# A retention block and a leaky-ReLU feed-forward block: the decay tables read from 8 rows, the first weights moved up in the load order, the first dense step cut by batch

## The chip, the cores and the metric

The kernel runs on one core of one Trainium2 chip. The core has a matrix engine (TensorE, "PE" in the profile, with its weight loads "PEld"), a vector engine (VectorE, "DVE"), a scalar engine (ScalarE, "ACT"), GpSimd ("POOL") and SyncE ("SP"). Each runs its own list of instructions in order, and they wait for each other through semaphores. Transfers between the main memory (HBM) and the on-chip memory (SBUF) run on 16 DMA engines; here SP issues nearly all of them and ACT issues two. Matrix products are summed in PSUM[...]. The metric is the device time of one execution, in microseconds, as the median of several runs.

## The reference

The inputs are q, k and v in float32, each of 4 batches, 8 heads, 768 positions and 64 dimensions, and w_in of 512 x 2048 and w_out of 2048 x 512 in float64. The kernel turns the weights into float32 itself.

```python
gamma = 1.0 - 2.0 ** (-5.0 - np.arange(H))
for t in range(S):
    state = gamma * state + k[t] (outer) v[t]        # per batch and head
    y[t] = scale * (q[t] @ state)
x = y as (B*S, H*D)                                  # 3072 x 512
h = x @ w_in
out = maximum(0.01 * h, h) @ w_out
```

The recurrence is computed in six chunks of 128 positions. Within a chunk, a product of q and k gives 128 x 128 scores, which are masked below the diagonal and multiplied with v; a factor of gamma to the power of the position goes onto v before (the table of v's decay) and onto the result after (the table of q's decay). Across chunks a state is carried.

## The kernel before, in words

The two dense layers take nearly all of the time. They are done chunk by chunk (4 batches x 128 positions = 512 tokens at a time) and, over the hidden dimension, in four units of 512. Most of them use a seven-product scheme for 2 x 2 blocks (Strassen's), and the later chunks a second level of it. The order of all instructions on every engine is written out by hand in the program; no planner decides it. Each engine takes its instructions in the order in which the program states them.

The change touches only the opening, the first chunk of attention and the first dense unit (about the first 17 us of the profile). What happens there, in the order of the code:

- **Loads** (lines 882 to 901). SP issues, in this order: q and k of batch 0, q and k of batch 1 (512 KB each, `load_qk`), v of batch 0 and of batch 1 (256 KB each, `load_v`), then the first two pieces of weights (`load_piece`, 512 KB each), then q and k of batch 2, v of batch 2, pieces 2 and 3, batch 3, and later the keys. ACT issues one small load, the decay tables, 8 rows of 948 float32 numbers.
- **Zeroing** (lines 884 to 886). The decay tables land in rows 0 to 7 of a tile `t` that is read over all 128 rows, so that the 948 columns are first set to zero, half of them by POOL and half by DVE. The load of the tables waits for that. DVE also zeroes a small piece (`nothing`), which feeds the products below.
- **Products of zeros** (`keep_busy(10)`, lines 914 and 931). PE multiplies zeros ten times while it waits for the first data.
- **Tables** (lines 934 to 938 and 946). PE spreads the 8 rows of decay factors over 128 partitions with three small products into a bank `tables`, and with one 512 wide product into a bank `spread`. ACT copies the first to `dec` (line 941; it holds the factors for v) and the second to `dec` too (line 950; the factors for the result).
- **Attention of chunk 0 by batch.** `score` (line 196, PE) makes the scores of a batch, `masked` (line 216, DVE) masks them, `decay_v` (line 163, POOL) scales v, `values` (lines 266 and 255, PE) multiplies scores and v, and `taken` (line 311, DVE) writes the result, scaled by q's decay, as the input x of the dense layer.
- **Weights from float64.** A piece becomes float32 through three steps of ACT (`next_powers`, lines 595, 599, 600) and three of DVE (`begin_mantissas` with lines 607 and 612, `end_mantissas` with line 619).
- **First dense unit** (`direct`, line 701). It computes two batches of chunk 0 with plain products in four steps; a step multiplies one piece of weights with 256 tokens (batches 0 and 1) into two banks, two products for each. A float32 product counts as two records in the profile, so that a step is 8 records. The program calls one step at a time (`next(steps)`), so that the steps stand between the scores and values of the later batches.

Before the change, PE's order in the opening is: ten products of zeros, scores 0, the three small tables, scores 1, spread, values 0, values 1, scores 2, dense step 0, dense step 1, values 2, scores 3, dense step 2, and so on.

Of the kernel before, what the change touches and what calls it, by code (L numbers as in the profile page):

```python
# [15 lines left out]
AF = mybir.ActivationFunctionType  # L16
# [6 lines left out]
def kernel(  # L23
# [14 lines left out]
    nc = tc.nc  # L38
    NC = S // C
    DM = H * D  # L40
    HP = H // 2
    NU = DF // 512
    N = B * C // 2
# [15 lines left out]
    dec = const.tile([128, HP * C + NC * H + HP], FP32, name="dec")  # L59
# [27 lines left out]
    def block(k, i):  # L87

        if k < N_UNITS - 1:
            return unit(k)[:, PLACE.get(i, i) if k % 2 else i]  # L90
        return units[k][i // 2][:, i % 2] if i < 6 else last_s4[:, 0]
# [3 lines left out]
    step = dec[:, HP * C + NC * H :]  # L95
# [24 lines left out]
    def load_qk(c, b, queue=nc.sync):  # L120
        queue.dma_start(out=heads[c, b][0], in_=qk[c, b])

    def load_v(c, b, queue=nc.sync):
        queue.dma_start(out=heads[c, b][1][:, 1], in_=kv[c, b][:, 1])
# [35 lines left out]
    def decay_v(c, b, engine=nc.gpsimd, behind=None):  # L160
        v = vals[c, b] if c >= JOINED else heads[c, b][1][:, 1]
        if engine is not nc.scalar:
            op = engine.tensor_tensor(out=v, in0=v,  # L163
                                      in1=gk[c].unsqueeze(2).to_broadcast([128, H, D]),
                                      op=ALU.mult)
            if behind is not None:
                tc.add_manual_dep(op.ins, behind.ins.name, IN_ORDER, reason="one port for both")
        else:
            for h in range(H):
                engine.activation(v[:, h], v[:, h], AF.Identity, scale=gk[c][:, h : h + 1])  # L170
# [9 lines left out]
    def score(c, b):  # L180

        ps = two_banks(f"ap_{c}_{b}").rearrange("p j a t -> p j (a t)")[:, :, 0:NS]
        scores[c, b] = ps.rearrange("p j (m n t) -> p j m n t", n=3, t=C // 2)
        scores_to(heads[c, b][0], [scores[c, b][:, j] for j in range(2)])
# [29 lines left out]
    def masked(c, b):  # L214
        am = new_am(c, b)
        nc.vector.tensor_tensor(
            out=am.rearrange("p j m n t -> p j m (n t)"),
            in0=scores[c, b].rearrange("p j m n t -> p j m (n t)"),
            in1=mask.rearrange("p n t -> p (n t)").unsqueeze(1).unsqueeze(1)
                .to_broadcast([128, 2, HP // 2, 3 * C // 2]), op=ALU.mult)  # L220
        scores[c, b] = am
# [20 lines left out]
    def values(c, b):  # L242
        if (c, b) not in sums_at:
            sums_at[c, b] = apart(two_banks(f"yp_{c}_{b}"))
        last_values(c, b)
        first_values(c, b)
# [51 lines left out]
    def taken(c, b, xb):  # L298

        tokens_taken(c, b, xb)  # L300
        state_taken(c, b, for_state(sums_at[c, b]))
# [232 lines left out]
    def load_piece(n, place=None):  # L534
        if n >= N_PIECES:
            return
        if not f64:
            nc.sync.dma_start(out=piece(n), in_=weights[n].rearrange("p (h n) -> p h n", h=2))
            return
        if place is None:  # L540
            tag, bufs = ("raw", 3) if n < N_PIECES - 4 else (("qk", "kv")[n % 2], AHEAD)
            raws[n] = work.tile([128, W], I64, tag=tag, bufs=bufs, name=f"raw{n}")
        else:
            raws[n] = place.bitcast(I64)
        nc.sync.dma_start(out=raws[n], in_=weights[n])

    def next_powers(scratch=None, between=None):
        n = done["powers"]
        done["powers"] += 1
        if n < N_PIECES and f64:  # L550
            powers(n, scratch, between)
        elif between is not None:
            between()

    def begin_mantissas(between=None):

        mantissas_begun(done["mantissas"], between)

    def end_mantissas():
        n = done["mantissas"]  # L560
        done["mantissas"] += 1
        op = mantissas_ended(n)
        if n != 3:
            load_piece(n + 4 if n < 3 else n + 3)
        if n == N_PIECES - 1:
            new_pair(2)
            for b in range(2):
                heads[2, b] = [work.tile([128, 2, HP, C], FP32, tag="qk", bufs=AHEAD,
                                         name=f"qk_2_{b}")]
            load_qk(2, 0)  # L570
            load_qk(2, 1)
            of_pair(2, 0, 1)
            of_pair(2, 0, 0)
        if n % 4 == 3 and n > 7:
            add_sums(n // 4)
        return op
# [121 lines left out]
    def temp(name, at):  # L698
        return work.tile([128, 2, N], FP32, tag=name, name=f"{name}_{at}")

    def direct(c, u, x, g, th):

        banks = [ffs.tile([128, 2, N], FP32, tag="ff", bufs=4, name=f"d{r}_{c}_{th}")
                 for r in range(2)]
        for step in range(4):
            kh, k = divmod(step, 2)
            for r in range(2):
                for i in range(2):
                    nc.tensor.matmul(  # L709
                        banks[r][:, i, :], lhsT=block(2 * u, r + 2 * kh)[:, k, ts(i, 128)],  # L710
                        rhs=x[:, 2 * kh + th, k, :], start=(step == 0 and i == 0),
                        stop=(step == 3), skip_group_check=True)
                if step == 3:
                    nc.scalar.activation(g[:, 2 * r + th], banks[r], AF.Prelu, alpha=0.01)
            yield

    filled = mask.rearrange("p n t -> p (n t)").bitcast(BF16)[:, 0:C]

# [157 lines left out]
    words = tile_x("words").rearrange("p i k n -> p (i k n)")[:, 0 : 2 * W]  # L876
    xs = {0: new_x(0)}
    x, t = xs[0]
    rows = t[:, 1:3].rearrange("p i k n -> p (i k n)")[:, 0 : decay.shape[1]]
    nothing = t[:, 0, 0, 0:64].bitcast(BF16)  # L880
    half = decay.shape[1] // 2
    load_qk(0, 0)
    load_qk(0, 1)
    nc.vector.memset(t[:, 0, 0, 0:64], 0.0)
    nc.gpsimd.memset(rows[:, :half], 0.0)
    nc.vector.memset(rows[:, half:], 0.0)
    nc.scalar.dma_start(out=rows[0:H], in_=decay)
    load_v(0, 0)
    load_v(0, 1)
    load_piece(0)  # L890
    load_piece(1)
    load_qk(0, 2)
    load_v(0, 2)
# [10 lines left out]
    for s in range(2):  # L904
        part = mask[ts(s, 64), 0 : 3 - s : 2 - s]
# [4 lines left out]
    parts = [new_g(0, 0)]  # L910
# [3 lines left out]
    def keep_busy(n):  # L914
        for _ in range(n):
            nc.tensor.matmul(idle.rearrange("p i (two n) -> p (i two) n", two=2), lhsT=nothing,
                             rhs=nothing.unsqueeze(1).to_broadcast([128, 4, 128]),
                             start=True, stop=True, skip_group_check=True)

    tables = ffs.tile([128, 2, N], FP32, tag="ff", bufs=4, name="tables")  # L920
    spread = ffs.tile([128, 2, N], FP32, tag="ff", bufs=4, name="spread")
    n_gq = HP * C
    ends = [0]
    for n in (C, C, NC * H, C, n_gq, HP):
        ends.append(ends[-1] + n)
    by_head, in_order, powers_of, place, g_q, g_step = (
        rows[:, i:j] for i, j in zip(ends, ends[1:]))
    def scratch(name, n):
        return work.tile([128, 2, N], FP32, tag=name, name=f"{name}_x{n}")

    keep_busy(10)
    score(0, 0)
    n_gk, n_old = NC * H, JOINED * H
    nc.tensor.matmul(tables[:, 0, 0:n_old], lhsT=by_head, rhs=powers_of[:, 0:n_old], start=True,
                     stop=True, skip_group_check=True)
    nc.tensor.matmul(tables[:, 0, n_old:n_gk], lhsT=in_order, rhs=powers_of[:, n_old:],
                     start=False, stop=True, skip_group_check=True)
    nc.tensor.matmul(tables[:, 0, n_gk : n_gk + HP], lhsT=place, rhs=g_step, start=False,
                     stop=True, skip_group_check=True)
    masked(0, 0)  # L940
    nc.scalar.copy(out=dec[:, n_gq:], in_=tables[:, 0, 0 : n_gk + HP])
    decay_v(0, 0)
    score(0, 1)
    decay_v(0, 1)
    masked(0, 1)
    nc.tensor.matmul(spread.rearrange("p i n -> p (i n)"), lhsT=place, rhs=g_q, start=True,
                     stop=True, skip_group_check=True)
    values(0, 0)
    values(0, 1)
    nc.scalar.copy(out=dec[:, 0:n_gq], in_=spread.rearrange("p i n -> p (i n)"))  # L950
    next_powers(scratch("m5", 0))
    begin_mantissas(lambda: taken(0, 0, x))
    taken(0, 1, x)
    end_mantissas()
    next_powers(scratch("u2", 1))
    score(0, 2)
    steps = direct(0, 0, x, parts[0][1], 0)
    next(steps)
    converted = next_mantissas()
    decay_v(0, 2, behind=converted)  # L960
# [41 lines left out]
    steps = direct(0, 0, x, parts[0][1], 1)  # L1002
# [171 lines left out]
    for u in range(NU):  # L1174
        for c in range(2) if u > 0 else ():
            if c == 0:
                parts = []
            parts.append(new_g(c, u))
            at = rounds(1, 3)
            at = put(at, **hidden_more.get((c, u), {}))  # L1180
            run(hidden(c, u, *xs[c], *parts[c][1:]), at)
        for c in range(2 if u < NU - 1 else 1):
            if u == 0:
                os[c] = new_o(c)
            at = rounds(1, 4 - c) if u < NU - 1 else {}
            at = put(at, **output_more.get((c, u), {}))
# [3 lines left out]
    banks = ctx.enter_context(tc.tile_pool(name="banks", bufs=1, space=bass.MemoryType.PSUM))  # L1190
# [406 lines left out]
    for n in range(N2):  # L1597
        c, u = at_of(n)
# [20 lines left out]
        part = gs.pop(n)  # L1619
# [183 lines left out]
```

## Time and profile before

| | |
|---|---|
| median of 3 runs | 628.3 us (628.2 to 628.65) |
| the profiled execution | 627.76 us |
| its span (first to last instruction) | 625.9 us |
| PE busy | 620.0 us, 99% of the span |
| DVE busy | 520.0 us, 83% |
| ACT busy | 285.5 us, 46% |
| POOL busy | 147.4 us, 24% |
| HBM traffic | 113.54 MB read, 26.48 MB written, 224 GB/s over the span |
| PE busy from 0 to 4.7 us / 4.7 to 12.2 us / 12.2 to 22.3 us | 3.65 / 5.62 / 10.04 us |
| PE busy from 22.3 to 60 us | 37.70 of 37.70 us |

Times inside the profile are counted from the start of the span. A group's row gives the busy time of the instructions of one line, with the idle time just before them and what ended it. "Landing" is the time at which the last part of a transfer has counted up its semaphore. PE's records overlap, because a product's end is modelled while the next one has begun, so that distances are best taken from start to start. The 1.86 us between the span and the profiled execution's own time lie outside the first and last instruction.

### The profile page before, as it was taken

Reading aid. Unit: us, or ns where it says so; the run is one execution under the profiler, and the core shown is the slowest. Engines: PE = TensorE matmul, PEld = TensorE weight load, DVE = VectorE, ACT = ScalarE, POOL = GpSimd, SP = SyncE. Lnnn points to the kernel's source line nnn. Section 1 sums busy time; section 2 is a strip of 40 time slices with the busy share of each in tenths; the row PEclk is TensorE's granted clock in tenths of the full one; section 3 lists DMA queues with packets and bytes.
Section 4 is the critical chain, followed back from the end, with each engine's and each line's share of the span. In section 5 each row is a group of like instructions: output and inputs, shape, how many; then the busy total and the mean of one; then the engine's idle time right before and its main releaser. Section 6 shows DMA issues by size and latency. Waiting matters only on the chain.

```text
span 625.9 us, 15366 instructions
## 1 busy us (share of the span) xinstructions
PE 620.0 (99%) x6410; PEld 571.8 (91%) x6410; DVE 520.0 (83%) x799; ACT 285.5 (46%) x546; POOL 147.4 (24%) x152
## 2 busy tenths in 40 slices
PE   8999999999999999999999999999999999999998
PEld 5888888888888889998999999999999999999997
DVE  5689769889979976779888868789968789989897
ACT  4876556347444114352433433634614435545641
POOL 2000000000010110105133052331250711379473
PEclk9999999999999999999999999999999999999999
DMA  8941426547772996496976996988478568688601
GB/s 324 403 154 42 127 68 215 159 144 231 259 282 75 327 362 248 130 349 198 334 232 205 292 335 235 327 277 283 148 262 268 174 226 266 207 276 290 206 3 67
DMA packets 105940, 141.00 MB, mean 225 GB/s; under 512 B 4488, under 2 KB 84232, under 8 KB 105872
## 3 DMA queue, kind: packets, MB, share of 16 engines
q1 hardware_dynamic: 105712, 139.94, 67.2%
q8 instruction: 50, 0.82, 0.5%
q14 instruction: 18, 0.15, 0.1%
q10 hardware_dynamic: 160, 0.10, 0.0%
HBM read 113.54 MB, written 26.48 MB: 224 GB/s over the span
## 4 chain that ended last, share of the span: by engine, by line
PE 98%; DMA 1%; DVE 0%; issue 0%; DVEq 0%
PE bank L1497 28%; PE bank L1342 14%; PE bank L688 10%; PE bank L1457 8%; PE C_h L688 4%; PE B_o L688 4%; PE A_h L688 4%; PE C_o L688 4%; PE A_o L688 4%; PE B_h L688 4%; PE d L709 2%; PE D_h L688 2%; PE D_o L688 2%; PE bank L374 1%; PE bank L456 1%; PE bank L385 1%
## 5 line engine op out<-in xcount | busy, mean ns | idle before, releaser
L623 DVE TENSOR_TENSOR made<-made,bank 128x512 f32<-128x512 f32 (+1 forms) x96 | 55.8, 617 | 33.0 <-PE bank L1497 29.3
L1497 PE MATMUL bank<-x,wb 128*128 128x128 f32 x672 | 78.5, 276 | 0.0
L1497 PEld LDWEIGHTS bank<-x,wb 128*128 128x128 f32 x672 | 77.3, 192 | 1.2 <-ACT bank L1501 0.2
L626 DVE TENSOR_TENSOR g<-g 128x512 f32<-128x512 f32 x96 | 66.0, 708 | 4.7 <-ACT g L1539 0.5
L1497 PE MATMUL bank<-x,wa 128*128 128x128 f32 x512 | 67.7, 275 | 0.0
L1497 PEld LDWEIGHTS bank<-x,wa 128*128 128x128 f32 x512 | 62.7, 192 | 0.3
L1501 ACT COPY bank<-bank 128x512 f32<-128x512 f32 (+1 forms) x32 | 16.6, 518 | 92.0 <-PE bank L1497 88.3
L623 DVE TENSOR_TENSOR g<-made 128x512 f32<-128x512 f32 x64 | 51.8, 830 | 3.3 <-DVE made L623 0.5
L1497 PE MATMUL bank<-t,wa 128*128 128x128 f32 x384 | 53.3, 275 | 0.0
L1342 PE MATMUL bank<-g,w 128*128 128x128 f32 x392 | 50.5, 276 | 0.0
L1497 PEld LDWEIGHTS bank<-t,wa 128*128 128x128 f32 x384 | 48.0, 192 | 0.0
L1342 PEld LDWEIGHTS bank<-g,w 128*128 128x128 f32 x392 | 46.8, 192 | 0.1
L1539 ACT ACTIVATE g<-g 128x512 f32<-128x512 f32 x64 | 38.1, 634 | 7.6 <-DVE g L623 7.6
L688 PE MATMUL bank<-g,w 128*128 128x256 f32 x168 | 38.0, 382 | 0.0
L1312 POOL TENSOR_TENSOR x<-g 128x512 f32<-128x512 f32 x12 | 17.0, 1419 | 88.9 <-DVE x L626 34.4
L1457 PE MATMUL bank<-g,w 128*128 128x256 f32 x168 | 37.8, 382 | 0.0
L163 POOL TENSOR_TENSOR in<-in,dec 128x512 f32<-128x512 f32 x3 | 3.7, 1232 | 144.2 <-DMA in<-in_kv_dram 139.2
L1457 PEld LDWEIGHTS bank<-g,w 128*128 128x128 f32 x168 | 31.4, 190 | 4.3
L688 PEld LDWEIGHTS bank<-g,w 128*128 128x128 f32 x168 | 31.3, 190 | 4.2
L623 DVE TENSOR_TENSOR o<-o,bank 128x512 f32<-128x512 f32 (+2 forms) x43 | 26.2, 632 | 10.2 <-ACT bank L806 4.3
L420 POOL MEMSET between<- 128x1 f32 x16 | 1.9, 117 | 130.8 <-PE bank L456 102.4
L623 DVE TENSOR_TENSOR o<-o,w 128x2048 f32<-128x2048 f32 (+2 forms) x16 | 27.4, 1731 | 0.2
(283 smaller groups left out, 1348.4 us busy)
## 6 DMA issues: line engine op xcount, KB each, us to landing
wa<-kept SPq DMA_DIRECT2D x16, 1344.0 KB, 8.5
w<-leaf_kept SPq DMA_DIRECT2D x44, 448.0 KB, 5.0
raw<-in_weights_dram SPq DMA_DIRECT2D x31, 512.0 KB, 4.3
wb<-kept SPq DMA_DIRECT2D x16, 896.0 KB, 6.3
wa<-kept SPq DMA_DIRECT2D x16, 448.0 KB, 4.6
wb<-kept SPq DMA_DIRECT2D x16, 448.0 KB, 6.9
out_dram<-o SPq DMA_DIRECT2D x23, 256.0 KB, 3.3
qk<-in_qk_dram SPq DMA_DIRECT2D x11, 512.0 KB, 8.2
```

Source lines behind the costliest of these rows:

```text
L374: nc.tensor.matmul(at[j][ts(h, 64), n, m, i], lhsT=x[ts(j, 64), 1, a, ts(h, 64)], rhs=x[ts(j, 64), 0, a, ts(h, 64)], start=(n == 0 and a = ...
L385: nc.tensor.matmul(sums[h][ts(j, 64), n, a], lhsT=key[ts(h, 64), 2 * a + j], rhs=val[ts(h, 64), 2 * a + j], start=(n == 0 and a == 0), sto ...
L623: return nc.vector.tensor_tensor(out=out, in0=a, in1=b, op=ALU.add)
L626: return nc.vector.tensor_tensor(out=out, in0=a, in1=b, op=ALU.subtract)
L688: nc.tensor.matmul(to, lhsT=block(w, sa)[:, k, ts(i, 128)], rhs=rhs[:, k, a:z], start=(first and (i == 0 or split) and n == 0 and k == 0), ...
L709: nc.tensor.matmul(banks[r][:, i, :], lhsT=block(2 * u, r + 2 * kh)[:, k, ts(i, 128)], rhs=x[:, 2 * kh + th, k, :], start=(step == 0 and i ...
L1312: op = nc.gpsimd.tensor_tensor(out=out, in0=a, in1=b, op=ALU.subtract)
L1342: nc.tensor.matmul(ps[q][:, to], lhsT=weights[i][j], rhs=moving[i][s], start=(i == 0 and m in ("M1", "M5", "M4")), stop=True, skip_group_c ...
L1457: nc.tensor.matmul(room[x][:, i, :], lhsT=block(2 * u + 1, sa)[:, k, ts(i, 128)], rhs=rhs[:, k, :], start=(first and i == 0 and k == 0), s ...
L1497: nc.tensor.matmul(ps[q][:, i], lhsT=w[:, j, i], rhs=part_of(moving[i], s), start=(i == 0 and m in ("M1", "M5", "M4")), stop=True, skip_gr ...
L1501: nc.scalar.copy(out=ps[3], in_=ps[0])
L1539: nc.scalar.activation(g[:, i], g[:, i], AF.Prelu, alpha=0.01)
```

## The change

Four things change, all in the opening.

1. The decay tables are read over their 8 rows alone: `rows` is `t[0:H, ...]`, and the two zeroing instructions of 474 columns are gone. The load of the tables no longer waits for them, and ACT issues it first thing.
2. The order of the loads on SP is now: q and k of batch 0, v of batch 0, weights piece 0, q and k of batch 1, v of batch 1, weights piece 1, and on as before.
3. The order of the work on PE is now: nine products of zeros (one fewer), scores 0, the three small tables, spread, values 0, scores 1, values 1, the first half of dense step 0 (batch 0), scores 2, the second half of dense step 0 (batch 1), dense step 1, values 2, scores 3, and on as before. A dense step that is cut has four products of 128 tokens in each half, and so twice the instructions.
4. The other engines follow. DVE now has mask 0, the first two weight steps of piece 0 (lines 607 and 612), `taken` of batch 0, mask 1, the third weight step (line 619), `taken` of batch 1, then piece 1. Before it had mask 0, mask 1, line 607, `taken` 0, line 612, `taken` 1, line 619, then piece 1. ACT copies the small tables ahead of everything and the spread table right behind, as before. POOL scales v of batch 0 and then of batch 1, as before.

From dense step 1 on, the order of the instructions on every engine and in every queue is that of before.

```diff
     def temp(name, at):
         return work.tile([128, 2, N], FP32, tag=name, name=f"{name}_{at}")
 
-    def direct(c, u, x, g, th):
+    def direct(c, u, x, g, th, by_batch=False):
 
         banks = [ffs.tile([128, 2, N], FP32, tag="ff", bufs=4, name=f"d{r}_{c}_{th}")
                  for r in range(2)]
         for step in range(4):
             kh, k = divmod(step, 2)
-            for r in range(2):
-                for i in range(2):
-                    nc.tensor.matmul(
-                        banks[r][:, i, :], lhsT=block(2 * u, r + 2 * kh)[:, k, ts(i, 128)],
-                        rhs=x[:, 2 * kh + th, k, :], start=(step == 0 and i == 0),
-                        stop=(step == 3), skip_group_check=True)
-                if step == 3:
-                    nc.scalar.activation(g[:, 2 * r + th], banks[r], AF.Prelu, alpha=0.01)
-            yield
+            n_parts = 2 if by_batch and step == 0 else 1
+            for part in range(n_parts):
+                at = ts(part, N // n_parts)
+                for r in range(2):
+                    for i in range(2):
+                        nc.tensor.matmul(
+                            banks[r][:, i, at], lhsT=block(2 * u, r + 2 * kh)[:, k, ts(i, 128)],
+                            rhs=x[:, 2 * kh + th, k, at],
+                            start=(step == 0 and part == 0 and i == 0),
+                            stop=(step == 3), skip_group_check=True)
+                    if step == 3:
+                        nc.scalar.activation(g[:, 2 * r + th], banks[r], AF.Prelu, alpha=0.01)
+                yield
 
     filled = mask.rearrange("p n t -> p (n t)").bitcast(BF16)[:, 0:C]
 
...
     words = tile_x("words").rearrange("p i k n -> p (i k n)")[:, 0 : 2 * W]
     xs = {0: new_x(0)}
     x, t = xs[0]
-    rows = t[:, 1:3].rearrange("p i k n -> p (i k n)")[:, 0 : decay.shape[1]]
+    rows = t[0:H, 1:3].rearrange("p i k n -> p (i k n)")[:, 0 : decay.shape[1]]
     nothing = t[:, 0, 0, 0:64].bitcast(BF16)
-    half = decay.shape[1] // 2
     load_qk(0, 0)
+    nc.scalar.dma_start(out=rows, in_=decay)
+    nc.vector.memset(t[:, 0, 0, 0:64], 0.0)
+    load_v(0, 0)
+    load_piece(0)
     load_qk(0, 1)
-    nc.vector.memset(t[:, 0, 0, 0:64], 0.0)
-    nc.gpsimd.memset(rows[:, :half], 0.0)
-    nc.vector.memset(rows[:, half:], 0.0)
-    nc.scalar.dma_start(out=rows[0:H], in_=decay)
-    load_v(0, 0)
     load_v(0, 1)
-    load_piece(0)
     load_piece(1)
     load_qk(0, 2)
     load_v(0, 2)
...
     def scratch(name, n):
         return work.tile([128, 2, N], FP32, tag=name, name=f"{name}_x{n}")
 
-    keep_busy(10)
+    n_gk, n_old = NC * H, JOINED * H
+    keep_busy(9)
     score(0, 0)
-    n_gk, n_old = NC * H, JOINED * H
     nc.tensor.matmul(tables[:, 0, 0:n_old], lhsT=by_head, rhs=powers_of[:, 0:n_old], start=True,
                      stop=True, skip_group_check=True)
     nc.tensor.matmul(tables[:, 0, n_old:n_gk], lhsT=in_order, rhs=powers_of[:, n_old:],
                      start=False, stop=True, skip_group_check=True)
     nc.tensor.matmul(tables[:, 0, n_gk : n_gk + HP], lhsT=place, rhs=g_step, start=False,
                      stop=True, skip_group_check=True)
+    nc.scalar.copy(out=dec[:, n_gq:], in_=tables[:, 0, 0 : n_gk + HP])
     masked(0, 0)
-    nc.scalar.copy(out=dec[:, n_gq:], in_=tables[:, 0, 0 : n_gk + HP])
     decay_v(0, 0)
+    nc.tensor.matmul(spread.rearrange("p i n -> p (i n)"), lhsT=place, rhs=g_q, start=True,
+                     stop=True, skip_group_check=True)
+    nc.scalar.copy(out=dec[:, 0:n_gq], in_=spread.rearrange("p i n -> p (i n)"))
+    values(0, 0)
+    next_powers(scratch("m5", 0))
+    begin_mantissas()
+    taken(0, 0, x)
     score(0, 1)
     decay_v(0, 1)
     masked(0, 1)
-    nc.tensor.matmul(spread.rearrange("p i n -> p (i n)"), lhsT=place, rhs=g_q, start=True,
-                     stop=True, skip_group_check=True)
-    values(0, 0)
+    end_mantissas()
     values(0, 1)
-    nc.scalar.copy(out=dec[:, 0:n_gq], in_=spread.rearrange("p i n -> p (i n)"))
-    next_powers(scratch("m5", 0))
-    begin_mantissas(lambda: taken(0, 0, x))
+    steps = direct(0, 0, x, parts[0][1], 0, by_batch=True)
+    next(steps)
     taken(0, 1, x)
-    end_mantissas()
     next_powers(scratch("u2", 1))
     score(0, 2)
-    steps = direct(0, 0, x, parts[0][1], 0)
     next(steps)
     converted = next_mantissas()
     decay_v(0, 2, behind=converted)
```

## The prediction

> **What bounds the kernel now.** I read the page's busy shares first (PE 99%), then PE's list of waits over the whole span, which has three entries.
>
> ```profile
> PE ap L196 <- DVE x L311: 1.1, 1, 1.1
> PE idle L916 <- DVE t L884: 1.1, 1, 1.1
> PE tables L934 <- DMA t<-decay_dram: 0.8, 1, 0.8
> ```
>
> All three lie in the first 12.3 us. The table of stages confirms it: from 22.3 us PE is busy 37.70 of 37.70 us, then 179.98 of 180.00 and 374.98 of 375.00. So PE's list is a rigid block from 12.26 us on, and a change of the opening is worth exactly what it moves that block. I therefore read PE's timeline of the opening (start, length, engine, line, operation):
>
> ```profile
> 4.71 0.90 PE L196 MATMUL ap<-qk 64*64 64x128 f32 x32
> 6.41 0.37 PE L934 MATMUL tables<-t 128*128 128x16 f32 x2 [0.80 <-DMA t<-decay_dram]
> 7.98 1.12 PE L946 MATMUL spread<-t 128*128 128x512 f32 x2
> 9.03 0.69 PE L266 MATMUL yp<-am,kv 128*64 128x64 f32 x16
> 10.04 0.69 PE L266 MATMUL yp<-am,kv 128*64 128x64 f32 x16
> 12.26 0.90 PE L196 MATMUL ap<-in 64*64 64x128 f32 x32 [1.14 <-DVE x L311]
> 13.09 3.72 PE L709 MATMUL d<-x,w 128*128 128x256 f32 x16
> 16.74 0.69 PE L266 MATMUL yp<-am,in 128*64 128x64 f32 x16
> 17.64 0.85 PE L196 MATMUL ap<-in 64*64 64x128 f32 x32
> ```
>
> Two holes are to be seen, 0.80 us at 5.61 and 1.14 us at 11.11. The second is credited to DVE's `taken` 1 (end 12.14), but scores 2 also need q and k of batch 2, issued at 3.67 with 8.5 us to landing, so 12.1: a tie that DMA makes too. The transfers themselves are full from about 3 us: 365 GB/s mean from 4.7 to 12.2 us, 402 from 12.2 to 22.3. Landings (issue plus time to landing): qk0 4.4, qk1 6.1, v0 6.9, v1 8.3, piece 0 9.6, piece 1 10.8, qk2 12.1, qk3 17.3. The last one matters: scores 3 run at 17.64, only 0.3 behind qk3. The chain that ended last begins with the tables:
>
> ```profile
> 1.59 4.69 DMA t<-decay_dram
> ```
>
> and DVE and POOL show the lengths that I need:
>
> ```profile
> 8.13 0.96 DVE L216 TENSOR_TENSOR am<-ap,mask 128x768 f32<-128x768 f32 x1 [1.41 <-PE ap L196]
> 12.65 0.42 DVE L607 TENSOR_SCALAR w<-raw 128x512 uint32<-128x512 uint32 x1
> 13.91 0.69 DVE L619 SCALAR_TENSOR_TENSOR w<-w,z 128x512 f32<-128x512 f32 x1
> 14.68 1.04 POOL L163 TENSOR_TENSOR in<-in,dec 128x512 f32<-128x512 f32 x1 [5.04 <-DVE w L619]
> 15.38 0.62 DVE L607 TENSOR_SCALAR w<-raw 128x512 uint32<-128x512 uint32 x1
> ```
>
> **What the Trainium skill says.** "TensorE: Matmul & The Clock Gate", Part 1: PE starts at half clock and is released after about 3.4 us of activity, in a free-running window; an idle window throttles it again. The trace agrees on the first half: the products of zeros start 0.43 us apart until about 3.6 us and 0.22 apart from about 4.0. The same page, "LDWEIGHTS": a weight load costs by its columns, not its rows, so tables of 8 rows are no cheaper on PE; the trace of before has only 128-row table loads (0.19 us). "SBUF — State Buffer", "Who interferes with whom": a DVE instruction with two SBUF inputs, or in a two-port mode, contends with POOL's reads. The trace agrees: line 607 took 0.62 us beside POOL's scaling and 0.42 without. "DMA: Bandwidth & Descriptors", "Issuing engines are not separate DMA queues": ACT's load shares the 16 engines with SP's. The trace agrees: the 30 KB of tables took 4.69 us behind SP's megabyte.
>
> **The change part by part.** Prices come from the rows above; hand-overs from the trace: PE to DVE 0.14, ACT to POOL 0.15, others to PE 0.13.
>
> *One product fewer*: 0.22 us at the late rate. Scores 0 now wait for qk0 alone (4.39 + 0.13): 4.53 instead of 4.71.
>
> *Tables.* Zeroing (0.49 on POOL, 0.45 on DVE) leaves; the load goes from 1.59 to about 0.8 and lies beside qk0. Bounds: landed before 5.36, which costs nothing, or again a transfer later, near 6.3, which costs 0.9. I take the first, since half a megabyte fewer is ahead of it. Its 30 KB at 400 GB/s delay qk0 by under 0.1; if ACT's issue (0.60 us) goes ahead of SP's, by up to 0.6.
>
> *The chain.* Scores 0 at 4.53; tables 0.83 later (as spread behind scores 1), 5.36; ended 0.80 later, 6.16; ACT's copy 0.20 with hand-overs, POOL at 6.55; scaling 1.04, 7.59; values 0 at 7.73 (spread, 6.03 to 7.15, fits ahead). Its length is 1.08: `taken` 0 from 8.95 to 9.64. Scores 1 follow values 0 on PE at 8.73 (values are 1.01 start to start), end 9.62; mask 1 from 9.77 to 10.73; values 1 at 10.86, ended 11.94; `taken` 1 from 12.08 to 12.77; only then, in DVE's order, piece 1: the three steps took 1.95 (12.65 to 14.60), so from 12.80 to 14.75. Dense step 1 can start at 14.88.
>
> *PE in between.* Half step 0 from 11.87 (line 619 of piece 0 is done at 11.45), scores 2 at 12.77, the second half at 13.6, ended near 14.5, and a hole of 0.4 us for piece 1. Cutting costs nearly nothing: 56 products of 128 columns take 6.25 us (0.112 each), 24 of 256 columns 5.18 (0.216), so 16 x 0.112 against 8 x 0.216 is 0.06 us, inside the hole; with the hole gone it is 0.06 on the path.
>
> *The sum.* Before, dense step 1 began half way between 13.09 and 16.74, at 14.92. After: 14.88. So values 2 come at 16.70 instead of 16.74, scores 3 at 17.60, and the rigid block moves by 0.04 us. PE's holes (0.58 ahead of values 0, 1.24 ahead of values 1, 0.4 ahead of step 1) hold what the old ones (0.80 and 1.14) and the removed product held. The work of dense step 0 went into the old hole, but the time came back as serialisation: batch 1's scores now stand behind batch 0's values on PE, and behind it mask, values and `taken` follow in series before piece 1 is converted.
>
> *The moved loads.* SP issues the same eight transfers first; nothing is added. v0 is needed by 6.55 and estimated at 4.4 + 0.8 = 5.2; piece 0 by about 7.8 (6.5); qk1 by 8.6 (7.8); v1 by 9.7 (about 9.0); piece 1 and qk2 land as before. All hidden by 0.6 us or more. POOL's first scaling now stands at 6.55 beside lines 607 and 612: below nothing is excluded, 0.2 us on DVE is free (`taken` 0 waits until 8.95), and if DVE comes first POOL waits up to 0.4 (a line 607) or 0.7 (a line 612), which is on the chain.
>
> From the profiled execution: 627.76 - 0.04 = 627.7. The median lies 0.54 above it, so 628.26; with the delays above more likely than gains I say **628.3 us**.
>
> **The rivals.**
>
> *All of PE's holes are gained* (0.80 + 1.14 + 0.22 = 2.2, to 626.1). For it: the dense half step fits into the hole at 11.1. Against it: scores 3 need qk3 at 17.3, so the block can move by at most about 0.2, unless the transfers come earlier too. They could by about 1 us: v0 and v1 took 2.2 us for 512 KB where others took 1.3. Then the chain above would still hold PE. A part of it, 0.2 to 0.9 us, to 627.4 to 628.1, is the likelier form.
>
> *The chain is later* by 0.3 to 1.0 us: tables or qk0 late from the shared DMA start, or POOL stretched by DVE. 628.6 to 629.3. For it: margins of 0.2 to 0.6 us only.
>
> *PE's clock falls back.* Between 7.15 and 10.86 PE now has 1.9 us of work in 3.7 us, where it had 5.6 in 7.5. If a whole window counts as idle, PE runs at half speed for another 3.4 us: 1.7 us more, 630.0, slower. It decides from a window of 3.4 us with too little activity; against it, before had a hole of 1.14 us and PE kept its full clock, and the new longest hole is 1.24.
>
> *The change does not do what it says*: the first weights do land earlier, but piece 1, which gates step 1, does not; this is inside my forecast.
>
> **How the numbers follow.** No net change (-0.3 to +0.3): 0.62. A partial gain of 0.3 to 1.2: 0.11. The later chain: 0.19. The clock: 0.05. Gain beyond 1.26 us: 0.02; another loss: 0.01. A measurement of this kernel tells about 0.2%, 1.26 us, from no change, so same 0.92, slower 0.06, faster 0.02. The range, 627.6 to 629.1, leaves out the clock, the largest gains and the far end of the later chain.
>
> **What would show it.** Right: PE starts scores 0 near 4.5, the wait for the tables' load is gone, holes of about 0.6 and 1.2 us stand ahead of line 266 (ended by POOL's scaling and by mask 1), and scores 3 start within 0.3 us of 17.6. Step by step: tables' first product 5.4, POOL's scaling 6.55, `taken` 1 at 12.1, line 619 of piece 1 ended by 14.8. Wrong: scores 3 at 17.4 or earlier with all later rows shifted alike (gain), tables after 6 us or scaling longer than 1.04 us (later chain), products of 256 columns 0.43 apart between 11 and 15 us (clock).

## The result and the profile after

The changed kernel takes **630.9 us** (median of 6 runs, 630.71 to 632.35), against 628.27 us for the kernel before in the same comparison (6 runs, 627.65 to 628.65). The ratio is 1.0046, with a 95% interval of [1.0033, 1.0059]: 2.6 us slower. The prediction, 628.3 us and no change, was wrong. The profiled execution of the changed kernel took 630.88 us, with a span of 629.1 us (625.9 before), so that it stands at the median, and the 3.2 us of its span are what has to be explained.

PE's list of waits in the changed kernel (instruction, what released it, us in total, times, longest) is the one that was forecast:

```profile
PE yp L266 <- DVE am L216: 1.2, 1, 1.2
PE idle L917 <- DVE t L887: 1.1, 1, 1.1
PE yp L266 <- POOL kv L163: 0.5, 1, 0.5
```

The wait for the tables' load is gone, and two holes of 0.51 and 1.19 us stand ahead of values 0 and values 1 (forecast: 0.58 and 1.24). Together the holes are shorter than before (1.70 us against 1.94). A reader who stopped here would call the kernel unchanged. PE's timeline of the changed kernel (start, length, engine, line, operation) says otherwise:

```profile
1.05 4.02 PE L917 MATMUL idle<-t 128*128 128x512 bf16 x9 [1.05 <-DVE t L887]
5.00 1.45 PE L196 MATMUL ap<-qk 64*64 64x128 f32 x32
6.38 0.39 PE L935 MATMUL tables<-t 8*128 8x16 f32 x2
7.07 1.10 PE L944 MATMUL spread<-t 8*128 8x512 f32 x2
8.69 0.69 PE L266 MATMUL yp<-am,kv 128*64 128x64 f32 x16 [0.51 <-POOL kv L163]
9.58 1.47 PE L196 MATMUL ap<-qk 64*64 64x128 f32 x32
12.25 1.12 PE L266 MATMUL yp<-am,kv 128*64 128x64 f32 x16 [1.19 <-DVE am L216]
13.94 2.07 PE L712 MATMUL d<-x,w 128*128 128x128 f32 x8
15.94 1.11 PE L196 MATMUL ap<-in 64*64 64x128 f32 x32
16.99 2.89 PE L712 MATMUL d<-x,w 128*128 128x128 f32 x16
19.80 0.69 PE L266 MATMUL yp<-am,in 128*64 128x64 f32 x16
20.70 0.85 PE L196 MATMUL ap<-in 64*64 64x128 f32 x32
```

The same products have other lengths. Scores 1 (9.58) take 1.47 us where scores 3 (20.70) take 0.85; values 1 take 1.12 and values 2 take 0.69. Values 2 start at 19.80 instead of 16.74 and scores 3 at 20.70 instead of 17.64: 3.06 us late, and still 3.1 us late at the end of the span. The table of stages shows why. Its columns are the stretch, its length, the busy time of PE, PEld, DVE, ACT and POOL (with instructions), the granted clock, the DMA share and GB/s:

```profile
6.30:9.60 3.30, 2.79 (x53) 1.82 (x49) 2.64 (x3) 1.56 (x4) 1.04 (x1) 1.00 0.99 367
9.70:13.00 3.30, 2.11 (x51) 1.94 (x44) 2.25 (x3) 2.89 (x5) 1.04 (x1) 0.50 1.02 402
13.00:16.40 3.40, 3.40 (x42) 2.94 (x42) 2.18 (x4) 0.61 (x2) 0.00 (x0) 0.50 1.03 407
16.60:22.30 5.70, 5.70 (x110) 4.92 (x99) 4.05 (x7) 4.94 (x13) 1.04 (x1) 1.00 1.05 406
```

The trace's record of the granted clock has PE at half from 9.62 to 16.45 us. That is two windows of 3.41 us, right after the first window at full clock (6.21 to 9.62). The kernel before, in its own stretches of nearly that length, stays at full clock:

```profile
7.40:10.70 3.30, 3.30 (x86) 2.25 (x78) 1.84 (x3) 1.58 (x4) 2.04 (x2) 1.00 1.02 407
10.80:14.10 3.30, 2.16 (x53) 1.86 (x51) 3.16 (x7) 2.62 (x5) 0.00 (x0) 1.00 1.04 413
```

Here is the riddle. The stretch that lost the clock (6.30 to 9.60, the first row of the changed kernel) has PE busy for 2.79 of 3.30 us. The stretch before the change from 10.80 to 14.10 has 2.16 of 3.30 us and kept it. Busy time doesn't tell which window is lost. What differs is the shape: in the lost window 1.8 us of the busy time are the tables and spread, which the timeline shows as `8*128`, products over 8 rows of the array.

This is not one bad execution. The mean granted clock that is listed with every execution was 0.995 in five of the six runs and 0.991 in one; no execution of the kernel before for which it is listed was below 0.999. One window at half clock is 3.41 x 0.5 = 1.7 us of 629, or 0.27%; so 0.997, 0.995 and 0.992 or 0.991 mean one, two and three windows. "Kept its clock" below means 0.999 or 1.0.

### The profile page after: what moved, and what is told of

The parts are those of the page before. It is cut to its first block, busy times and chain, and to the rows that moved or that the text cites. A ratio compares the mean times of both kernels' runs of the same rounds, so it can differ in the third digit from the quotient of the medians.

```text
span 629.1 us, 15378 instructions
## 1 busy us (share of the span) xinstructions
PE 623.3 (99%) x6417; PEld 574.8 (91%) x6417; DVE 520.1 (83%) x798; ACT 285.8 (45%) x546; POOL 146.6 (23%) x151
## 4 chain that ended last, share of the span: by engine, by line
PE 99%; DVE 0%; POOL 0%; issue 0%; ACT 0%; POOLq 0%
PE bank L1500 28%; PE bank L1345 14%; PE bank L688 10%; PE bank L1460 8%; PE C_h L688 4%; PE B_o L688 4%; PE A_h L688 4%; PE C_o L688 4%; PE A_o L688 4%; PE B_h L688 4%; PE d L712 3%; PE D_o L688 2%; PE D_h L688 2%; PE ap L196 1%; PE bank L456 1%; PE bank L374 1%
```

## The experiments

Three theories stood at the start. **Rows**: products over 8 rows count for little of what holds the clock, so the removed zeroing (that is, the reading of 128 rows) is what costs. **Order**: the new order of the work spreads PE's work too thin, whatever the rows. **Chain**: the serial chain through scores, mask and values got longer, and the clock is a by-product.

| kernel | rows of the tables | loads on SP | order on PE | runs | kept the clock | median us (range) | ratio to before [95%] |
|---|---|---|---|---|---|---|---|
| changed | 8 | new | new | 6 | 0 | 630.9 (630.71 to 632.35) | 1.0046 [1.0033, 1.0059] |
| e7, changed again | 8 | new | new | 4 | 0 | 631.42 (631.13 to 632.31) | 1.0051 [1.0034, 1.0068] |
| e5 | 8, loaded late | new | new | 4 | 0 | 631.58 (630.55 to 631.64) | 1.0051 [1.0036, 1.0066] |
| e6 | 64, loaded late | new | new | 8 | 3 | 631.79 (628.6 to 633.37) | 1.005 [1.0031, 1.0069] |
| e1 | 128, loaded late | new | new | 12 | 12 | 628.89 (628.36 to 629.96) | 1.0013 [1.0005, 1.0022] |
| e9 | 8 | new | old | 6 | 1 | 631.37 (628.43 to 632.52) | 1.005 [1.0034, 1.0065] |
| e8 | 128, loaded late | new | old | 10 | 6 | 629.17 (628.69 to 631.17) | 1.0025 [1.0015, 1.0035] |
| e3 | 8 | old | old | 12 | 11 | 628.24 (627.52 to 628.82) | 1.0002 [0.9994, 1.0011] |
| e4 | 128, nine products of zeros | old | old | 12 | 11 | 628.13 (627.61 to 629.77) | 1.0002 [0.9993, 1.001] |
| e2 | 8, with six more products of zeros | new | new | 20 | 17 | 629.0 (627.69 to 630.68) | 1.0015 [1.0008, 1.0023] |
| e10 | as e5, with the six | new | new | 4 | 2 | 630.13 (629.57 to 632.13) | 1.0039 [1.0025, 1.0053] |
| e11 | 128, q and k of batch 2 sooner | old | old | 13 | 13 | 628.19 (627.95 to 628.93) | 1.0003 [0.9995, 1.0011] |
| e12 | 128, products of zeros over 8 rows | old | old | 4 | 4, see below | 630.89 (630.46 to 631.87) | 1.005 [1.0033, 1.0067] |

"Loaded late" means that the tile is zeroed and the load waits for it, as before the change. All of these kernels compute the whole reference.

**e1: 128 rows again.** The changed kernel with the zeroing and the reading of 128 rows put back, and with them the late load.

```diff
-    rows = t[0:H, 1:3].rearrange("p i k n -> p (i k n)")[:, 0 : decay.shape[1]]
+    rows = t[:, 1:3].rearrange("p i k n -> p (i k n)")[:, 0 : decay.shape[1]]
...
-    nc.scalar.dma_start(out=rows, in_=decay)
     nc.vector.memset(t[:, 0, 0, 0:64], 0.0)
+    nc.gpsimd.memset(rows[:, :half], 0.0)
+    nc.vector.memset(rows[:, half:], 0.0)
+    nc.scalar.dma_start(out=rows[0:H], in_=decay)
```

> The changed kernel with the decay tables read over 128 zeroed rows again, everything else as changed. Theory R (the granted clock follows how many rows of the array work, and the tables and spread over 8 rows count for nearly nothing): PE keeps full clock once it has it, the half-clock stretch from 9.62 to 16.45 us is gone, and the time is about 628.3 to 629.0. Theory O (it is the new order with its two holes that lets the clock fall, whatever the rows): the half-clock stretch stays and the time stays at 630.9. Theory S (the clock is a side show and the serial chain costs the time): 630.9 or more, even where the clock is full.

It took 628.89 us, and all 12 executions kept the clock. PE's timeline of e1:

```profile
4.50 0.90 PE L196 MATMUL ap<-qk 64*64 64x128 f32 x32
5.94 0.37 PE L938 MATMUL tables<-t 128*128 128x16 f32 x2 [0.54 <-DMA t<-decay_dram]
8.38 0.69 PE L266 MATMUL yp<-am,kv 128*64 128x64 f32 x16 [0.68 <-POOL kv L163]
9.28 0.85 PE L196 MATMUL ap<-qk 64*64 64x128 f32 x32
11.32 0.69 PE L266 MATMUL yp<-am,kv 128*64 128x64 f32 x16 [1.19 <-DVE am L216]
17.07 0.69 PE L266 MATMUL yp<-am,in 128*64 128x64 f32 x16
```

Scores 1 are back at 0.85 us and values 1 at 0.69, though the holes (0.54, 0.68 and 1.19) are longer than those of the changed kernel. So neither the new orders of work and loads nor their waits cost the clock by themselves. The chain is the forecast one: from the tables to values 0 2.44 us (forecast 2.37), from values 0 to values 1 2.94 (3.13), from values 1 to values 2 5.75 (5.84). It only begins 0.58 us later, because the tables' load lands at 5.80. Values 2 are 0.33 us later than before (17.07 against 16.74). The median is 0.8 us above that of before (1.0005 to 1.0022); later small waits, of 0.3 and 0.2 us, show in its list of waits, and the rest was not traced further.

**e5: the rows alone.** As e1, with the zeroing and the late load kept, but the products read 8 of the rows. Against e1 one line differs:

```diff
     by_head, in_order, powers_of, place, g_q, g_step = (
-        rows[:, i:j] for i, j in zip(ends, ends[1:]))
+        rows[0:H, i:j] for i, j in zip(ends, ends[1:]))
```

> As the run with 128 rows (zeroing kept, the tables' load waits for it), but the products read 8 rows of what lies there. It separates the rows from the later load and its zeroing. Theory R (rows): the clock falls back again, 630.5 to 631.3. If instead the early load of the tables caused the fall: full clock and 628.9 as with 128 rows.

It took 631.58 us, 2.7 us more than e1, and no execution kept the clock. The table of stages of e5 answers to that of the changed kernel:

```profile
6.30:9.60 3.30, 2.63 (x40) 1.66 (x35) 2.70 (x3) 1.53 (x4) 1.81 (x2) 1.00 0.99 362
9.70:13.00 3.30, 2.11 (x57) 1.94 (x50) 2.25 (x3) 2.83 (x5) 0.57 (x1) 0.50 1.02 392
```

The rows that the four table products read are the only difference to e1, so in this order of work and loads they are the cause. The early load of the tables, which the change also brings, is not needed for it. The time is a little above theory R's range (630.5 to 631.3). e1 and e5 ran on different chips, which took 628.12 and 628.05 us for the kernel before. The chip does not explain the difference: e10, which is e5 with six more products of zeros, ran on e1's chip and lost the clock in 2 of 4 executions, where e1 lost it in none of 12.

**e6: 64 rows.** The edit of e1 with `t[0:64, ...]`, so that 64 rows are zeroed and read.

> The same with 64 rows zeroed and read. Theory R with an activity that grows with the rows: between, so that the clock falls back in some runs and not in others, 628.9 to 631. A rule by the whole array alone: as with 8 rows, 630.5 to 631.3.

Three of 8 executions kept the clock (628.6, 629.42 and 629.78 us), three lost two windows and two lost three (631.57 to 633.37). It lies between 8 rows (0 of 14 with this order) and 128 (12 of 12): the effect is graded in the rows. The slow executions lie above the expected range (628.9 to 631).

**e7: the changed kernel again**, without an edit.

> The changed kernel itself beside the other two, on their chip. Theory R: 630.7 to 631.1, with a half-clock stretch of one or two windows of 3.4 us in every run, wherever the first release falls. Theory P (chance of the moment at which the window starts): times spread between 628.5 and 632 with the release.

It fell back in 4 of 4. In its profile the first release came at 4.94 us, not at 6.21, and the clock was lost one window later all the same (8.35 to 18.59, three windows). So the fall is no accident of where the windows lie, and theory P, a spread from 628.5 us on, did not come. All four times lie above theory R's range (630.7 to 631.1); in the profile three windows are lost where it allowed for two.

**e9: the order undone.** The changed kernel with the orders of PE, DVE and ACT of before, its 8 rows, early load and new loads on SP kept. The part of the edit that moves scores 1 back:

```diff
     score(0, 0)
...
     decay_v(0, 0)
+    score(0, 1)
+    decay_v(0, 1)
+    masked(0, 1)
     nc.tensor.matmul(spread.rearrange("p i n -> p (i n)"), lhsT=place, rhs=g_q, start=True,
                      stop=True, skip_group_check=True)
...
-    score(0, 1)
-    decay_v(0, 1)
-    masked(0, 1)
```

> The changed kernel with the order of PE, DVE and ACT of before (ten products of zeros, scores 1 between the tables and spread, the dense step uncut); its 8 rows, its early load of the tables and its order of loads are kept. So one edit of the change is undone, the order. If the rows and the order are both needed for the fall of the clock, full-clock work on 64 and 128 rows again stands between the 8-row products, and most executions keep the full clock: about 629.2, as the new loads alone cost (629.17), with the wait for q and k of batch 1 near 1 us ahead of scores 1. If the 8 rows are enough beside the later loads, because that wait too is a stretch with little work, most executions fall back and it takes 631 or more. If the loads do nothing on the clock and nothing on the chain, 628.2.

Five of 6 executions fell back (631.05 to 632.52 us); the one that didn't took 628.43. That is a miss for the first reading, in which the rows and the order are both needed; the second one, 8 rows beside the later loads, came true. Against e3 below, which has the old loads and kept the clock in 11 of 12 executions, the new loads do the order's part. They bring q and k of batch 1 later (8.03 us in its profile, 6.06 before), and scores 1, though early in the order again, wait for them. PE's list of waits in the profile of e9, which is of the execution that kept its clock:

```profile
PE idle L913 <- DVE t L883: 1.1, 1, 1.1
PE ap L196 <- DMA qk<-in_qk_dram: 1.0, 1, 1.0
PE d L709 <- DVE w L619: 0.9, 1, 0.9
```

**e8: the new loads alone**, on the kernel before, with its 128 rows.

```diff
     load_qk(0, 0)
+    load_v(0, 0)
+    load_piece(0)
     load_qk(0, 1)
...
-    load_v(0, 0)
     load_v(0, 1)
-    load_piece(0)
```

> The kernel before with the new order of the loads alone. All theories: the clock stays full. Scores 1 now come where q and k of batch 1 land, near 8 us instead of 7.15, but scores 2 still wait for 12.1, so 628.1 to 628.5.

It took 629.17 us, which misses the expectation twice, in the time and in the clock. Scores 1 wait 1.16 us for q and k of batch 1; four of 10 executions lose the clock even at 128 rows, mostly for one window. At full clock it still took 628.69 to 629.29. So the order of loads is a loss in itself with the old order of work; with the new order, which puts scores 1 behind values 0, e1 kept the clock every time.

**e3: the rows and the early load alone**, on the kernel before: the edit of e1 turned round.

> The kernel before with the first part of the change alone: tables over 8 rows, no zeroing, ACT's load first, all else as before. Theory R: spread (7.98 to 9.1 us) now counts for little, and the clock falls back in some or all runs, 629.5 to 631. Theory O: no change of the clock, 628.0 to 628.4. Theory S: the wait for the tables of 0.80 us goes but scores 2 still wait for their load, 628.3.

It took 628.24 us, no change, and 11 of 12 executions kept the clock. That misses theory R's expectation (629.5 to 631): 8 rows alone are not enough to lose it. With the old loads, scores 1 follow the tables without a wait, and in its profile PE has no hole until 11.4 us. PE no longer waits for the tables' load, yet scores 2 start no sooner than before (12.26 us):

```profile
5.43 1.29 PE L196 MATMUL ap<-qk 64*64 64x128 f32 x32
6.66 0.39 PE L931 MATMUL tables<-t 8*128 8x16 f32 x2
12.54 0.90 PE L196 MATMUL ap<-in 64*64 64x128 f32 x32 [1.16 <-DVE x L311]
```

In this execution the first release came at 6.32 us (3.92 before), so that the ten products of zeros and scores 0 ran mostly at half clock and filled the time in which PE had waited. The hole ahead of scores 2 stayed (1.16 us, 1.14 before).

**e4: nine products of zeros**, on the kernel before: `keep_busy(9)`.

> The kernel before with nine products of zeros instead of ten, all else as before. If the tenth product is what brings the clock up in time: a later release (after 6 us instead of 3.9) and 628.8 to 629.5. If the release follows a window that runs on its own: release at a time that differs from run to run, and 628.3 as before, since scores 2 wait for their load at 12.1 us in any case.

It took 628.13 us, no change, as forecast; one execution of 12 lost a window.

**e2 and e10: filling the holes.** Two products of zeros more ahead of values 0 and four ahead of values 1; they read 128 rows and nothing waits for their result. e2 has them in the changed kernel, e10 in e5.

```diff
+    keep_busy(2)
     values(0, 0)
...
+    keep_busy(4)
     values(0, 1)
```

> The changed kernel with six more products of zeros over 128 rows: two between spread and values 0, four between scores 1 and values 1, where PE only waits. Theories R and O: the clock is held at full after the first release and the time is about 628.3 to 629.0. Theory S: nothing is gained by work in the holes, 630.9 to 631.5.

> The kernel that zeroes and loads as before but reads 8 rows (631.58, every execution at a mean clock of 0.995), with two products of zeros more ahead of values 0 and four ahead of values 1. The products of zeros read 128 rows. If the activity of the array holds the clock, and products over 8 rows count for little of it, these six products (some 2.6 us at half clock, 1.3 at full) bring the full clock back in most executions: 628.3 to 629.2, and no execution at 0.995 or below, or few. If the fall comes from the order of the work alone, or from the waits themselves, nothing changes: 631.5. As the load of the tables is late here, it also tells whether the spread of the earlier filled kernel (627.7 to 630.7) came from the early load: then this one spreads by no more than 1 us.

In the changed kernel they bring the clock back in 17 of 20 executions, and the others lose one window instead of two or three: 629.0 us. In e5 they bring it back in 2 of 4. So array work of no use, added in the holes, protects the clock, though the kernel has no fewer waits. The expectation for e10 (628.3 to 629.2) was too good: even the two executions that kept their clock took 629.57 and 630.09. Why e2 spreads over 3 us while keeping its clock was not settled; with two such executions e10 can't decide it. In e2's profile (629.67 us) SP issued q and k of batch 1 at 3.30 us instead of 2.24, and scores 1 waited 0.67 us for them; whether that makes the spread is not shown.

**e11: a try at something faster.** The kernel before with q and k of batch 2 issued ahead of weights piece 1, because scores 2 waited until 12.26 us, when both that transfer and `taken` 1 came in.

> The kernel before with one transfer moved: q and k of batch 2 are issued ahead of the second piece of weights. This is a try at something faster. Scores 2 waited until 12.26 for q and k of batch 2 (12.12) and for the writing of x. If the transfer set that wait, scores 2 start when DVE has written x, which does not move, so nothing is gained: 628.2. If DVE's work moves too, up to 0.2 us is gained, since q and k of batch 3 land at 17.3 and scores 3 run at 17.64. If the second piece, 1.3 us later, holds dense step 1 instead, it is up to 0.5 slower.

It took 628.19 us, no change. In its profile scores 2 start at 11.29 with no wait, ahead of `taken` 1 (11.75 to 12.43). So they do not need `taken` 1: of the two that came in together before, the transfer set the wait, though the view named DVE. The hole now stands one instruction further, 0.90 us ahead of dense step 0, for the weights (line 619), so that nothing is gained. No version that beats the kernel before was found.

**e12: products of zeros over 8 rows.** This takes the question away from the change. Only the ten products of zeros at the start of the kernel before are altered:

```diff
-            nc.tensor.matmul(idle.rearrange("p i (two n) -> p (i two) n", two=2), lhsT=nothing,
-                             rhs=nothing.unsqueeze(1).to_broadcast([128, 4, 128]),
+            nc.tensor.matmul(idle.rearrange("p i (two n) -> p (i two) n", two=2), lhsT=nothing[0:H],
+                             rhs=nothing[0:H].unsqueeze(1).to_broadcast([H, 4, 128]),
```

> The kernel before with one edit: its ten products of zeros read 8 rows instead of 128. They still start 0.43 us apart at half clock, and nothing waits for what they make, so by busy time nothing changes. This tests the rows at the other end, the release of the full clock at the start, where no wait of the change plays a part. In the ten profiles so far the release came between 3.78 and 7.07 us, one window length apart at most. If products over 8 rows count for little activity, the release comes a window of 3.41 us later in most executions, between about 6 and 10.5 us, so that scores 0, the tables and often scores 1 and spread run at half clock; the two holes of 0.80 and 1.14 us take up a part, and it takes 628.6 to 630.5. If busy time counts whatever the rows, the release stays at or before 7.2 us and the time is 628.1.

It took 630.89 us, 2.9 us more than before (627.95 in that comparison), and slower than the expected range. The timeline of e12:

```profile
1.05 4.44 PE L916 MATMUL idle<-t 8*128 8x512 bf16 x10 [1.05 <-DVE t L884]
5.43 1.56 PE L196 MATMUL ap<-qk 64*64 64x128 f32 x32
6.92 0.61 PE L934 MATMUL tables<-t 128*128 128x16 f32 x2
8.29 1.56 PE L196 MATMUL ap<-qk 64*64 64x128 f32 x32
9.78 2.06 PE L946 MATMUL spread<-t 128*128 128x512 f32 x2
11.77 0.69 PE L266 MATMUL yp<-am,kv 128*64 128x64 f32 x16
19.31 0.69 PE L266 MATMUL yp<-am,in 128*64 128x64 f32 x16
```

PE is busy without a gap from 1.05 us until 14.6. Yet scores 0, scores 1 (1.56 us each) and spread (2.06) run at half clock, and the release comes at 11.69 us, where in the thirteen other profiles of this study it came between 3.78 and 7.07. (The mean clock of e12 is listed as 1.0 because the record of the clock begins with the first release; values 2, at 19.31 instead of 16.74, show the loss.) By busy time the three windows of 3.41 us ahead of 11.69 are all full, and busy time alone would have released it as before. The products over 8 rows count for little at the release as well as at the fall.

**What a window must hold.** From the traces of all these profiles I summed, per window of 3.41 us, PE's time from start to start (no longer than a product's recorded length), once plain and once with the tables, spread and products of zeros weighted by their rows over 128. The weight is an assumption, and all other products count in full: scores and a part of the values use 64 rows each, but 32 records of scores start within 0.83 us, 26 ns apart, where a record of 128 columns takes 112 ns by itself (6.25 us for 56), so that by this estimate several are under way in the array at once. The windows that begin at full clock and are the thinnest of their kernels:

| window of | us | busy | weighted by rows | then |
|---|---|---|---|---|
| e5 (8 rows) | 6.26 to 9.67 | 2.74 | 1.06 | half |
| changed (8) | 6.21 to 9.62 | 2.90 | 1.22 | half |
| e7 (8) | 4.94 to 8.35 | 2.90 | 1.22 | half |
| e6 (64) | 5.30 to 8.71 | 2.75 | 1.85 | half |
| e9 (8) | 5.42 to 8.83 | 2.43 | 1.65 | full |
| e3 (8) | 6.32 to 9.73 | 3.41 | 1.72 | full |
| e2 (8, filled) | 5.19 to 8.60 | 3.41 | 1.80 | full |
| e1 (128) | 7.19 to 10.61 | 2.25 | 2.25 | full |
| e8 (128) | 5.56 to 8.97 | 2.25 | 2.25 | full |
| before (128) | 10.75 to 14.16 | 2.27 | 2.27 | full |

e4, e10, e11 and e12 are left out; their thinnest windows at full clock hold 2.00 (e10) or more, weighted, and were kept. Plain busy time has it upside down (lost at 2.74 to 2.90, kept at 2.25). Weighted by rows, the lost windows lie at 1.06 to 1.22 and the kept ones at 1.65 and above, with one exception, e6. So the weight is not exactly the share of rows, or 1.65 to 1.85 is a zone where both happen. The windows lie elsewhere in each execution: laid from 6.27 us on, a window of e9's own profile would hold 0.93 (an estimate from its timeline), which suits the five executions of e9 that fell back. It does not suit e8, where no window after the release in its profile holds less than 2.25 and four of 10 executions lost the clock. The weighted sum tells 8 rows from 128; it is not the whole rule, and these runs can't tell what is missing.

## Why the prediction was wrong

Its steps, against the profiles.

- **The chain was right.** Measured at full clock in e1, its three legs are within 0.2 us of the forecast. In the changed kernel, from the tables to values 0 took 2.31 us (forecast 2.37). The first two holes stood where they were forecast, ended by what was forecast; the third, of 0.4 us ahead of dense step 1, is in the list of waits of neither kernel.
- **The tables' load was right, its worth was not.** It landed at 2.71 us and the wait is gone. The forecast then had the tables at 5.36; they came at 6.38. In that execution the first release fell at 6.21 us, so that nine products of zeros ran until 5.0 at 0.43 us each and scores 0 took 1.45. The forecast had taken the early release of the profile before (3.92) as given. So the sign that it gave for a later chain, tables after 6 us, appeared too, but from half-clock products and not from a late transfer. Before, such a late release was absorbed: in e11, released at 6.38, the tables are only 0.27 us later than in the profile before and values 2 0.37 us.
- **One product fewer, the cut step and the moved loads** cost nothing that shows in e4 or on the chain of e1. But the new loads alone (e8) are a loss of their own: with the old order of work they make PE wait 1.16 us, and they thin the windows. The forecast's "all hidden by 0.6 us or more" was about the new order of work, where e1 shows no wait for them; in e2 scores 1 waited 0.67 us.
- **The failed step is "PE's clock falls back"**, which the sum put at nothing and the list of rivals at a chance of 0.05. Its mechanism is what happened, and its mark, products of longer length between 11 and 15 us, is in the timeline. It was sized by PE's busy time and by the longest hole ("before had a hole of 1.14 us and PE kept its full clock, and the new longest hole is 1.24"). That is the wrong measure. It looked from 7.15 us on, behind the tables and spread, and so took their 1.8 us, now over 8 rows, for work like any other. The window that lost the clock, 6.21 to 9.62, takes them in: PE is busy for 2.90 us of it, and weighted by rows it holds 1.22. With 128 rows and nothing else altered (e1 against e5) the clock stayed. The remark that tables of 8 rows are no cheaper on PE held (a weight load of the tables took 0.187 us over 8 rows and 0.192 over 128, spread 1.10 and 1.12), and it hid the point: the same time buys less clock.
- **The size** was too small as well: one window, 1.7 us. It fell back for two (five of six runs) or three. In the profiled execution the 3.10 us by which values 2 were later than forecast (19.80 against 16.70) add up as: tables 1.02 late by the late release; -0.06 from the tables to values 0; 0.43 from values 0 to values 1 (scores 1 at half clock); 1.71 from values 1 to values 2 (7.55 against 5.84 us, at half clock until 16.45). Between executions of one kernel, e6 gives the price of two windows: 632.0 on average for 0.995 against 629.3 at full clock, 2.7 us.

The gains that the first rival spoke of did not come.

In the Trainium skill, "TensorE: Matmul & The Clock Gate" describes under "Part 1" a free-running window of about 3.4 us, and the traces agree (9.62 to 16.45 is twice 3.41, and the first release falls at another time in each profile, from 3.78 to 7.07 where the products of zeros read 128 rows). Its table under "Why this matters for your kernels" warns of idle gaps above some 3 us; here the measurement decides: the clock was lost by a window (6.21 to 9.62) whose only gap is the 0.51 us ahead of values 0.

## What to carry to other kernels

When a change makes a product narrower in rows, or thins out PE's first microseconds, weigh PE's work by the rows of the array that it uses, window by window, before calling the holes equal; the zeroing that let these tables be read over 128 rows cost 0.45 us of DVE and 0.49 of POOL and bought 2.7 us of clock (e1 against e5). Compare the length of one and the same product before and after the edit ahead of the list of waits, since a lost clock shows there and in no wait. And where a kernel needs its PE warm, products of zeros should cover the rows: over 128 they warmed it, over 8 they were worth next to nothing (e12).

## What the runs showed of the hardware that was not expected

- Products over 8 rows of the array keep PE busy as long as products over 128 (0.43 us at half clock, 1.10 against 1.12 us for spread), but they did not release the clock (e12: 11.69 us instead of at most 7.07), and a window made up of them and a little other work did not hold it (0 of 14 executions of the changed kernel, e5 and e7).
- In the changed kernel, e5, e6, e7 and e9 a clock once lost stayed lost for two or three windows although PE worked again (some executions of e2, e3, e4, e8 and e10 lost one alone, by their mean clock). In the profile of the changed kernel the window from 9.62 to 13.04 holds 2.21 us of work, about what the kernel before keeps its clock with (2.27).
- Products of zeros count: the six of e2 held the clock in 17 of 20 executions. The 120 rows that e1 has more than e5 hold zeros too, and they made the difference. So work on zeros counts.
